# Attention-output pieces in front of the score bursts, and one more piece kept back: a transformer block on one core

## The chip, the cores and the metric

The kernel runs on one core of one Trainium2 chip. The metric is the device time of one execution in microseconds (us), as the median of several runs. Engines: PE is the tensor engine's matmul, PEld its weight loads, DVE the vector engine, ACT the scalar engine, POOL GpSimd, SP the engine that issues the transfers here.

## The reference, cut to what matters

```python
# x: 1 x 2048 x 1024, bf16; 32 heads of 32; causal window of 256
qkv = layernorm(x) @ wqkv
scores = q @ k.T * 32 ** -0.5          # masked: 0 <= query - key < 256
h = x + (softmax(scores) @ v) @ wo
out = h + silu(layernorm(h) @ w1) @ w2 # w1: 1024 x 3584, w2: 3584 x 1024
```

## The kernel before: the parts concerned

The tokens are worked on in four blocks of 512. The dense matmuls of one block (QKV of the next block, or the output projection of the earlier ones) are interleaved with the attention of another, by hooks between single matmuls. A *burst* is a group of 16 to 24 score matmuls on 32-row tiles of the array; ACT then takes their exponentials and POOL sets the masked triangles to zero. A *piece* is 15 to 24 small matmuls (33 columns), which multiply those exponentials by v; DVE divides by the row sums. The last piece of a head schedules a DMA transpose of its output for the start of the next dense group.

The code is shortened here.

```python
class Stream:
    def __init__(self, b):
        self.bursts, self.pieces, self.done, self.given, self.seen = [], [], 0, 0, 0
        self.behind = 2 if b else 1
        pending.extend(coming); coming.clear()      # what the last stream left
        ...                                         # 20 bursts and pieces (16 in block 0)
    def between(self, kt):                          # ahead of each of 192 dense matmuls
        if self.seen * self.n >= self.done * 192:
            self.bursts[self.done]()
            self.done += 1
        if self.seen * self.n * 2 >= (self.given * 2 + 1) * 192:
            if pending:
                pending.pop(0)()
            coming.append(self.pieces[self.given])
            if len(coming) > self.behind:
                pending.append(coming.pop(0))
            self.given += 1
        self.seen += 1
```

Pieces that the last stream leaves over run in the next stage, the first feed-forward matmul, one behind each of its first groups. The projection of block 3 starts in that stage, behind group 6:

```python
run_late()                      # transposes that are due
load_w2(5)
for ft in range(FT):            # here for b == 0; extra: the pieces left over
    acc = h1_group(b, ft)
    run_late()
    if extra:
        extra.pop(0)[0]()
    if b == 0 and ft == 3:
        for i in (1, 2, 3, 4):
            load_w2(i)          # 1 MB each, on SP's queue, as the transposes are
    silu(b, acc, ft)
    if b == 0 and 6 <= ft < 14:
        wo_group(NB - 1, *divmod(ft - 6, 2))   # needs the transposes of all 8 head groups
```

The text calls a head group (four of the 32 heads) a head, as the prediction does: 0 to 7. [...] marks cuts above; the whole kernel may stand here:

The softmax here doesn't subtract the row's maximum and nothing guards it: scores larger than these inputs give would overflow.

## Time and profile before

| | before |
|---|---|
| time, median (the first three runs) | 693.31 us (693.14 to 693.49) |
| span of the profiled run | 691.4 us |
| PE busy, share of the span | 677.0 us, 98% |
| share of PE in the chain that ended last | 97% |
| waits of PE after the first 54 us | none with another engine as releaser |
| last small piece of the streams, start of the next stage | 285.01, 286.48 us |

The rows of the tensor engine at the end of the last stream, in front of those that the prediction shows (start, length, engine, line, operation, out<-in, shape, count):

```profile
283.56 0.43 PE L308 MATMUL sc<-r_a 32*64 32x320 bf16 x24
284.15 1.03 PE L276 MATMUL acc<-r_o,r_a 128*128 128x512 bf16 x4 [0.16 <-issue]
285.01 0.76 PE L388 MATMUL o_ps<-r_a,r_e 128*128 128x33 bf16 x24
285.61 1.02 PE L276 MATMUL acc<-r_o,r_a 128*128 128x512 bf16 x4
```

In the rows `sc` marks a burst, `o_ps` a piece, and `acc` or `hacc` dense matmuls. Read them by their starts: the modelled length of a dense matmul is 379 ns, but the next one starts after 215, so that lengths overlap. For the same reason an idle time shown in brackets behind a dense matmul is 0.16 us shorter than what was lost. The `[0.16 <-issue]` above is no such wait: there the record of one matmul is missing.

### The profile page before, as it was taken

Reading aid. Unit: us, or ns where it says so; the run is one execution under the profiler, and the core shown is the slowest. Engines: PE = TensorE matmul, PEld = TensorE weight load, DVE = VectorE, ACT = ScalarE, POOL = GpSimd, SP = SyncE. Lnnn points to the kernel's source line nnn. Section 1 sums busy time; section 2 is a strip of 40 time slices with the busy share of each in tenths; the row PEclk is TensorE's granted clock in tenths of the full one; section 3 lists DMA queues with packets and bytes.
Section 4 is the critical chain, followed back from the end, with each engine's and each line's share of the span. In section 5 each row is a group of like instructions: output and inputs, shape, how many; then the busy total and the mean of one; then the engine's idle time right before and its main releaser. Section 6 shows DMA issues by size and latency. Waiting matters only on the chain.

```text
span 691.4 us, 14107 instructions
## 1 busy us (share of the span) xinstructions
PE 677.0 (98%) x5895; PEld 331.6 (48%) x6011; DVE 290.5 (42%) x609; ACT 241.8 (35%) x463; POOL 160.4 (23%) x295
## 2 busy tenths in 40 slices
PE   8999999999999999999999999999999999999998
PEld 3444455555555555544444444444444444444445
DVE  5267646744444439534315133343133251333111
ACT  5326666766666666421310033300133100233000
POOL 1007666656666666500000000000000000000000
PEclk9999999999999999999999999999999999999999
DMA  8732242136241889971023410022300024100110
GB/s 251 251 55 78 39 80 61 26 63 183 73 131 17 241 235 281 213 277 50 12 80 111 93 39 0 1 91 69 85 0 1 17 95 95 39 1 1 30 39 24
DMA packets 76463, 60.95 MB, mean 88 GB/s; under 512 B 50288, under 2 KB 60528, under 8 KB 76400
## 3 DMA queue, kind: packets, MB, share of 16 engines
q1 hardware_dynamic: 76256, 59.78, 32.0%
q8 instruction: 47, 0.77, 0.5%
q10 hardware_dynamic: 144, 0.26, 0.1%
q14 instruction: 16, 0.13, 0.1%
HBM read 39.85 MB, written 8.39 MB: 70 GB/s over the span
## 4 chain that ended last, share of the span: by engine, by line
PE 97%; issue 1%; DMA 1%; SPq 0%; DVE 0%
PE hacc L628 19%; PE hacc L665 17%; PE acc L255 16%; PE acc L665 10%; PE acc L628 9%; PE acc L245 8%; PE acc L276 7%; PE o_ps L388 5%; PE sc L308 3%; PE hacc L276 1%; DMA r_w<-in_A_wqkv_dram 1%; PE sc L360 1%; PE sc L334 1%; PE tp L223 0%; SPq L135 0%
## 5 line engine op out<-in xcount | busy, mean ns | idle before, releaser
L378 POOL TENSOR_SCALAR_AFFINE_SELECT r_e<-r_e 128x512 bf16<-128x512 bf16 (+1 forms) x288 | 157.4, 561 | 126.6 <-ACT r_e L368 62.7
L665 PEld LDWEIGHTS <-r_a 128*128 128x128 bf16 x952 | 90.9, 98 | 103.0
L628 PEld LDWEIGHTS <-r_w 128*128 128x128 bf16 x896 | 87.4, 98 | 105.0 <-issue 0.2
L665 PE MATMUL hacc<-r_a 128*128 128x512 bf16 (+2 forms) x607 | 121.8, 359 | 0.5
L628 PE MATMUL hacc<-r_e,r_w 128*128 128x512 bf16 x444 | 99.7, 379 | 0.5
L320 ACT ACTIVATE r_e<-sc 128x768 bf16<-128x768 f32 x96 | 78.2, 814 | 48.3 <-PE sc L308 47.6
L637 ACT ACTIVATE r_n<-hacc 128x512 f32<-128x512 f32 x30 | 17.9, 597 | 178.9 <-PE hacc L628 175.5
L665 PE MATMUL acc<-r_a 128*128 128x512 bf16 x329 | 73.5, 379 | 0.4
L255 PEld LDWEIGHTS <-r_w 128*128 128x128 bf16 x512 | 44.2, 97 | 46.1 <-issue 1.0
L255 PE MATMUL acc<-r_t,r_w 128*128 128x512 bf16 x233 | 60.3, 379 | 2.4 <-issue 1.7
L257 DVE CAST r_a<-acc 128x512 bf16<-128x512 f32 x56 | 38.6, 690 | 56.6 <-PE acc L255 43.8
L255 PE MATMUL acc<-r_w 128*128 128x512 bf16 x240 | 58.0, 379 | 1.5 <-issue 0.9
L388 PEld LDWEIGHTS <-r_e 128*128 128x128 bf16 x1440 | 47.4, 96 | 17.9
L276 PE MATMUL acc<-r_o,r_a 128*128 128x512 bf16 x188 | 49.5, 379 | 1.9 <-issue 1.3
L628 PE MATMUL acc<-r_e,r_w 128*128 128x512 bf16 x213 | 48.9, 379 | 0.3
L388 PE MATMUL o_ps<-r_a,r_e 128*128 128x33 bf16 x1440 | 48.1, 178 | 0.1
L321 ACT ACTIVATE r_e<-sc 128x256 bf16<-128x256 f32 x96 | 37.6, 392 | 0.0
L680 DVE SCALAR_TENSOR_TENSOR r_t<-hacc,r_t 128x512 bf16<-128x512 f32 (+2 forms) x22 | 14.0, 635 | 55.2 <-PE hacc L665 53.8
L680 DVE SCALAR_TENSOR_TENSOR r_t<-acc,r_t 128x512 bf16<-128x512 f32 x12 | 8.3, 692 | 64.2 <-PE acc L665 58.8
L638 DVE SCALAR_TENSOR_TENSOR r_a<-r_n,hacc 128x512 bf16<-128x512 f32 x30 | 20.6, 688 | 33.0 <-ACT r_n L637 33.0
L628 PE MATMUL hacc<-r_a,r_w 128*128 128x512 bf16 x139 | 32.6, 379 | 0.3
L276 PEld LDWEIGHTS <-r_a 128*128 128x128 bf16 x256 | 21.8, 97 | 22.3
(79 smaller groups left out, 532.5 us busy)
## 6 DMA issues: line engine op xcount, KB each, us to landing
r_w<-in_B_w_dram SPq DMA_DIRECT2D x8, 896.0 KB, 5.2
r_a<-in_B_w_dram SPq DMA_DIRECT2D x7, 1024.0 KB, 7.5
r_w<-in_A_wqkv_dram SPq DMA_DIRECT2D x6, 1024.0 KB, 9.3
h_dram<-r_t SPq DMA_DIRECT2D x16, 256.0 KB, 2.5
r_t<-h_dram SPq DMA_DIRECT2D x16, 256.0 KB, 2.9
out_dram<-r_t SPq DMA_DIRECT2D x31, 128.0 KB, 1.7
r_o<-in_A_x_dram SPq DMA_DIRECT2D x15, 256.0 KB, 4.2
r_e<-h_dram SPq DMA_DIRECT2D x3, 1024.0 KB, 5.7
```

The source lines that it names most:

```text
L245: nc.tensor.matmul(acc, lhsT=lnT_b[b % 2][:, kt, j * P:(j + 1) * P], rhs=wv[:, kt, c * 512:(c + 1) * 512], start=(kt == 0), stop=(kt == KT ...
L255: nc.tensor.matmul(acc, lhsT=wqk[:, kt, col0:col0 + P], rhs=lnT_b[b % 2][:, kt, :], start=(kt == 0), stop=(kt == KT - 1))
L257: copy(out=(qT, kT)[which][b][:, g, :], in_=acc)
L276: nc.tensor.matmul(acc, lhsT=qT[b][:, g, j * P:(j + 1) * P], rhs=wo[:, g, c * 512:(c + 1) * 512], start=(g == 0), stop=(g == G - 1))
L308: nc.tensor.matmul(sc[hh // 2][half * 64:half * 64 + 64, hh % 2, col:col + qb - qa], lhsT=kT[t // 4][r0:r0 + DH, g, k0:k0 + 64], rhs=qT[b] ...
L320: nc.scalar.activation(out=tri[:, :, :, 64:256], in_=both, func=ACT.Exp, scale=scale)
L321: nc.scalar.activation(out=e[:, 1024:1280].rearrange("p (h q) -> p h q", q=P), in_=bank[:, :, 192:320], func=ACT.Exp, scale=scale)
L378: nc.gpsimd.affine_select(out=dst, in_=src, pattern=[[0, n] for n in dst.shape[1:-1]] + [[sgn, P]], compare_op=ALU.is_ge if upper else ALU ...
L388: nc.tensor.matmul(o_ps[pair][:, qt * 2 + hh, 0:VW], lhsT=chunk_of(i, bank, piece, pair, hh), rhs=v[:, b * 4 + kt, g * 4 + pair * 2 + hh, ...
L628: nc.tensor.matmul(acc, lhsT=w1[:, kt, ft * P:(ft + 1) * P], rhs=ln2T[b][:, kt, :], start=(kt == 0), stop=(kt == KT - 1))
L665: nc.tensor.matmul(acc[:, 0:c1 - c0], lhsT=gT[:, ft, j * P:(j + 1) * P], rhs=w2[ft // 4][:, ft % 4, c0:c1], start=(ft == 0), stop=(ft == F ...
L680: nc.vector.scalar_tensor_tensor(out=t_out[j % 2][:, c0:c1], in0=acc[:, 0:c1 - c0], scalar=0.5, in1=t_in[j % 2][:, c0:c1], op0=ALU.mult, o ...
```

## The change

The intent is to have fewer changes of kind on the tensor engine: each piece directly in front of a burst. With the position alone each piece would run half a slot sooner after its burst (3 slots, not 3.5), so it is kept back by one more.

```diff
-            self.behind = 2 if b else 1
+            self.behind = 3 if b else 2
 ...
             if self.seen * self.n >= self.done * 192:
-                self.bursts[self.done]()
-                self.done += 1
-            if self.seen * self.n * 2 >= (self.given * 2 + 1) * 192:
                 if pending:
                     pending.pop(0)()
-                coming.append(self.pieces[self.given])
+                self.bursts[self.done]()
+                coming.append(self.pieces[self.done])
                 if len(coming) > self.behind:
                     pending.append(coming.pop(0))
-                self.given += 1
+                self.done += 1
             self.seen += 1
```

More of the change, by code (lines that the diff above doesn't have):

```diff
@@ L424, in __init__ @@
         def __init__(self, b):
-            self.bursts, self.pieces, self.done, self.given, self.seen = [], [], 0, 0, 0
-            self.behind = 2 if b else 1
+            self.bursts, self.pieces, self.done, self.seen = [], [], 0, 0
+            self.behind = 3 if b else 2
             pending.extend(coming)
```

## The prediction

> **What bounds the kernel now.** I read four views in this order: the page (who is busy), the chain that ended last (what sets the end), the list of waits (is there one that a new order could remove), and then the timeline of the tensor engine inside a stretch where the change acts.
>
> From the page, engine totals and the chain:
>
> ```profile
> PE 677.0 (98%) x5895; PEld 331.6 (48%) x6011; DVE 290.5 (42%) x609; ACT 241.8 (35%) x463; POOL 160.4 (23%) x295
> ...
> PE 97%; issue 1%; DMA 1%; SPq 0%; DVE 0%
> ```
>
> The matmul engine is busy for 98% and 97% of the chain lies on it, so only what the tensor engine itself does, or waits for, counts. In the list of waits the longest entries belong to ACT, DVE and POOL, which wait for PE. For PE there is almost nothing after the start ("PE acc L255 <- issue" 2.7 us in 17 times; 0.16 us each, where the rows beside it lack one matmul, so I read these as missing records). So there is no wait to win. What is left is the cost of changing from one kind of matmul to another. The timeline of PE, two slots of it (columns: start, length, engine, line, operation, out<-in, shape, count):
>
> ```profile
> 200.35 0.38 PE L255 MATMUL acc<-r_t,r_w 128*128 128x512 bf16 x1
> 200.56 0.61 PE L388 MATMUL o_ps<-r_a,r_e 128*128 128x33 bf16 x18
> 201.03 1.24 PE L255 MATMUL acc<-r_t,r_w 128*128 128x512 bf16 x5
> 202.19 0.43 PE L308 MATMUL sc<-r_a 32*64 32x320 bf16 x24
> 202.78 0.81 PE L255 MATMUL acc<-r_t,r_w 128*128 128x512 bf16 x3 [0.16 <-issue]
> 203.43 0.54 PE L388 MATMUL o_ps<-r_a,r_e 128*128 128x33 bf16 x15
> 203.81 1.24 PE L255 MATMUL acc<-r_t,r_w 128*128 128x512 bf16 x5
> 204.99 0.43 PE L308 MATMUL sc<-r_a 32*64 32x320 bf16 x24
> ```
>
> Read start to start, since lengths overlap. Five dense matmuls in a row last 1.24 us with the last one 0.379 us long, so one starts every (1.24-0.38)/4 = 0.215 us. Dense to piece: three from 202.78 put the next start at 203.43, as found (203.43): no loss. Piece to dense: 18 small ones from 200.56 to 201.03 are 0.026 us each, 15 from 203.43 to 203.81 are 0.025: no loss either. Dense to burst: the fifth dense matmul started at 201.03+4x0.215 = 201.89 and would free the array at 202.11; the burst starts at 202.19, 0.09 us later. The same on 203.81: 204.89 against 204.99. Only entering a burst (and leaving it) costs something; a piece between dense matmuls is free of transition cost.
>
> **What the Trainium skill says.** "TensorE: Matmul & The Clock Gate", Step-by-step: what each phase is for: weight loads are pulled ahead of running matmuls if the row groups don't conflict or they go to the background buffer. The trace agrees for dense and piece (0.215 and 0.025 us, no gap) and shows that a burst's first load of a 32-row tile is not hidden (0.09 us). Same page, What's actually happening: a window of about 3.4 us without matmuls drops the clock to half. This trace has no idle gap of that length; it shows only the cold state at the start (the 11 warm-up matmuls take 632 ns in the mean against 379 later). "DMA: Bandwidth & Descriptors", Queues, rings and completion order: on each DMA engine the descriptors of one ring are taken in ring order, and a completion count lands only after all earlier writes of that engine. The trace agrees: an attention transpose issued right behind two 1 MB weight loads and two 256 KB ones landed after 8.7 us; one with a free queue takes 2.4 us (issued at 165.97 and 293.81):
>
> ```profile
> r_a<-r_n SPq DMA_TRANSPOSE x1, 8.7
> ```
> ```profile
> r_a<-r_n SPq DMA_TRANSPOSE x1, 2.4
> ```
>
> **The change part by part.** (a) Order. Before, a slot is burst, dense, piece, dense; after, piece, burst, dense. Piece p ran 3.5 slots behind its burst p, now 4 (blocks 1 to 3; 2.5 to 3 in block 0). Between two bursts there is therefore the same piece as before: burst k to burst k+1 held piece k-3 at k+0.5 and holds piece (k+1)-4 = k-3 now. So the time that ACT has to empty the score banks before the next burst is unchanged (it uses about 2.7 us of at least 2.79), and bursts stay where they were. No instruction is added or removed: 12,024 rows on PE in both.
>
> (b) Transitions. Per slot one dense-to-burst (0.215+0.09) and one piece-to-dense (0.026) are replaced by one piece-to-burst and one dense-to-dense (0.215). The loss of 0.09 us goes with entering the tiled mode, not with what ran before: leaving the burst costs about as much (a burst of 24 from 204.99 takes 0.35 us to the next dense start at 205.34, though its last matmuls have 64 columns). So piece-to-burst should be 33 columns at the dense rate, 0.215x33/512 = 0.014, plus 0.094, 0.108 us: 0.108+0.215-0.305-0.026 = -0.01 us. Of the 76 pieces, 13+19+20+20 = 72 still run in the four streams: 72 x -0.01 = -0.6 us in all.
>
> (c) The tail. Keeping back one more piece leaves four, not three, behind the last stream: the second half of head 6 (24 matmuls) and the three of head 7 (15, 18, 15). They run after the first four dense groups of the next stage. The transpose of head 7 is issued at the start of the group after its last piece, now the fifth group and no longer the fourth. But in the fourth group the program issues four 1 MB loads of the second weight. The instruction orders of the two kernels set side by side show it: on SP the row "transpose, then four loads" has become "four loads, then transpose". Output projection of block 3 needs that transpose at the eighth matmul of its first group, after seven groups. Before, timelines of PE and SP:
>
> ```profile
> 286.48 1.89 PE L628 MATMUL acc<-r_a,r_w 128*128 128x512 bf16 x8
> 288.20 0.53 PE L388 MATMUL o_ps<-r_a,r_e 128*128 128x33 bf16 x15
> ...
> 299.78 1.89 PE L276 MATMUL hacc<-r_o,r_a 128*128 128x512 bf16 x8
> ```
> ```profile
> 293.81 1.20 SPq L408 DMA_TRANSPOSE r_a<-r_n  x1
> 295.05 2.75 SPq L619 DMA_DIRECT2D r_a<-in_B_w_dram  x4
> ```
>
> First, the stage's start. The piece of 24 leaves the stream (24x0.0254 = 0.61 us), so the stage could begin at 286.48-0.61 = 285.87. But its first weight load needs the last of four layer-norm transposes, which was issued at 282.86 and landed after 3.3 us, at 286.2; I take 286.3, a loss of 0.4 us. Then the need: seven groups of 8x0.2155 (12.07), four pieces of 72 small matmuls (1.83) and seven matmuls (1.51) later: 286.3+15.4 = 301.7. (The same sum with three pieces gives 299.77 for the start of the first projection group before; the trace has 299.78.)
>
> When is it ready? Head 6's piece ends at 286.3+1.72+0.61 = 288.6; before, its transpose followed a piece by 0.94 us (292.87 to 293.81), so 289.6, and SP is free for the first of the four loads 1.24 us later, at 290.8. The last load waits on SP for the last piece, at about 295, which does not matter as the three before it fill the queue. Before, the last of the four landed 14.9 us after the issue of the first (296.82+13.1-295.05):
>
> ```profile
> r_a<-in_B_w_dram SPq DMA_DIRECT2D x1, 1024.0 KB, 13.1
> ```
>
> That gives 305.7, and 0.4 more for the transpose (in the case of 8.7 us it landed 0.4 after the load ahead of it): 306.1, a stall of 4.4 us. By the rate in the flat part of the DMA row (about 390 GB/s: 10.8 us for four, with 2.3 us before the first bytes and 0.6 for the transpose) it is ready at 304.5, a stall of 2.8. I take the middle, 3.6 us. PE works in order, has no slack afterwards, and nothing gives this back. A gap of this length may also just let the clock drop for one window; I estimate 1.7 us at a chance of about one in eight, 0.2.
>
> Sum: 693.3 - 0.6 + 0.4 + 3.6 + 0.2 = 696.9 us, +0.5%.
>
> **The rivals.** (1) The weight load of the burst hides under the small matmuls, and piece-to-burst costs 0.026 like piece-to-dense. Then 72 x 0.09 = 6.5 us are saved and the result is 691 us. For it: it is the obvious purpose of the change. Against it: leaving a burst costs the same 0.09 us although short matmuls precede. (2) The transposes don't stall: the loads may be issued early enough, or the first group may be late. Then about 693. Against it stand the 8.7 us above. (3) The pieces come later against ACT, POOL and DVE, and rings or banks fill: a score ring is freed by a piece one place in front of the burst that refills it, on the same engine, so the refill never waits; and waits for POOL's masks become shorter. I give it nothing. (4) The stall is long enough to cool the clock for longer, or the queue is slower than 280 GB/s: 699 to 701.
>
> **Range and chances.** The tail alone (2.8 to 4.4) gives 696.1 to 697.7; rival 1 in part and rival 2 pull down to 693, rival 4 up to 700: 693.0 to 699.8. A change of 2% would be 13.9 us. Saving that is twice what all transitions cost; losing it needs a queue twice as slow. Faster 0.01, same 0.97, slower 0.02.
>
> **What would show it.** In the changed profile: the first projection group of block 3 (the one at 299.78 before) is split by an idle of about 3.6 us whose releaser is a DMA into r_a from r_n; SP shows the four loads ahead of that transpose, which takes about 10 us to land; the stream's rows show piece to burst at 0.11 us start to start; bursts keep their times up to 283.6 within 1 us. The prediction is wrong if the burst follows the last small matmul after 0.03 us, or if no DMA wait stands before the projection.

## The result, and the profile after

The changed kernel took 699.27 us (699.0 to 699.84, 4 runs) against 693.24 us (4 runs): ratio 1.0089, 95% interval 1.0074 to 1.0103. A ratio here is the mean time of one kernel's runs over that of the other's in the same rounds, so it isn't quite the ratio of the medians. Its result is correct. It is 6.0 us slower; 3.6 were forecast.

Engine totals and the chain of the changed kernel, from its page:

```profile
PE 678.5 (97%) x5896; PEld 342.6 (49%) x6011; DVE 291.6 (42%) x609; ACT 241.8 (35%) x463; POOL 160.8 (23%) x295
...
PE 96%; DMA 2%; issue 1%; SPq 0%; DVE 0%
```

PE does the same work; the DMA share of the chain has gone from 1% to 2% (the page lists the new 1% as `DMA r_a<-r_n`, an attention transpose). First the streams, at the place that the prediction showed:

```profile
201.47 0.61 PE L388 MATMUL o_ps<-r_a,r_e 128*128 128x33 bf16 x18
202.01 0.43 PE L308 MATMUL sc<-r_a 32*64 32x320 bf16 x24
202.59 1.89 PE L255 MATMUL acc<-r_t,r_w 128*128 128x512 bf16 x8 [0.16 <-issue]
204.32 0.54 PE L388 MATMUL o_ps<-r_a,r_e 128*128 128x33 bf16 x15
204.79 0.43 PE L308 MATMUL sc<-r_a 32*64 32x320 bf16 x24
```

18 small matmuls at 0.0255 would put the burst at 201.93 if it followed as another small one does; it starts at 202.01, 0.08 later. In the trace's start times, the 72 steps from a last small matmul to a burst took 106 to 111 ns, against 309 to 312 from a dense one and 25 to 27 from a small matmul to a dense one (both in the kernel before). By these steps one slot gains 0.309+0.026-0.216-0.108 = 0.011 us, 0.8 us in 72 slots; the streams as a whole show less. The last burst of the streams began at 283.56 before and begins at 283.17 now; the first at 50.54 and 50.72. That makes -0.57 us over the streams, and +0.18 from the program's start, in which executions differ. The -0.57 is firm: from first to last burst the changed kernel and runs 1, 5, 6 and 7 took 232.45 us each, the kernel before and run 2 took 233.02. Where the other 0.2 of the 0.8 went I can't say.

Now the tail, tensor engine:

```profile
283.75 1.89 PE L276 MATMUL acc<-r_o,r_a 128*128 128x512 bf16 x8 [0.16 <-issue]
286.10 1.89 PE L626 MATMUL acc<-r_a,r_w 128*128 128x512 bf16 x8 [0.46 <-issue]
287.82 0.76 PE L388 MATMUL o_ps<-r_a,r_e 128*128 128x33 bf16 x24
...
300.00 1.68 PE L276 MATMUL hacc<-r_o,r_a 128*128 128x512 bf16 x7
305.89 0.39 PE L276 MATMUL hacc<-r_o,r_a 128*128 128x512 bf16 x1 [4.22 <-DMA r_a<-r_n]
306.12 2.81 PE L626 MATMUL hacc<-r_a,r_w 128*128 128x512 bf16 x8
```

and SP, with the time that the transpose issued at 295.71 took to land:

```profile
289.35 1.20 SPq L408 DMA_TRANSPOSE r_a<-r_n  x1
290.60 4.57 SPq L617 DMA_DIRECT2D r_a<-in_B_w_dram  x4
295.71 3.44 SPq L408 DMA_TRANSPOSE r_a<-r_n  x1
```
```profile
r_a<-r_n SPq DMA_TRANSPOSE x1, 10.1
```

The stage begins late (0.46 shown, 0.62 lost), the projection's first seven matmuls run, and the eighth waits for the transpose: 4.6 us from the seventh to the eighth, where 0.22 are due, so 4.38 lost. Then eight dense matmuls last 2.81 us and no longer 1.89: from 306.93 on they run at half the clock. The engines' shares in three stretches of the length of one clock record (stretch, its length, busy us of PE, PEld, DVE, ACT, POOL with counts, granted clock, DMA share, GB/s):

```profile
300.10:303.52 3.42, 1.57 (x8) 0.49 (x5) 0.69 (x1) 0.60 (x1) 0.00 (x0) 1.00 1.04 384
303.52:306.93 3.41, 1.04 (x5) 0.51 (x6) 0.61 (x1) 0.00 (x0) 0.00 (x0) 1.00 0.56 181
306.93:310.35 3.42, 3.42 (x9) 1.18 (x8) 0.77 (x2) 0.60 (x1) 0.00 (x0) 0.50 0.02 5
```

In the first two, PE is idle for more than half; the third is busy throughout but at 0.50. The kernel before in the same stretch ran 17 matmuls in place of 9:

```profile
306.93:310.35 3.42, 3.42 (x17) 1.54 (x16) 1.38 (x2) 0.56 (x2) 0.00 (x0) 1.00 0.53 196
```

3.41 us at half speed lose 1.70. The account: -0.57 (streams) +0.18 (start) +0.62 (late start of the stage) +4.38 (transpose) +1.70 (clock) = +6.31; the profiled spans are 691.4 and 697.7 us.

### The profile page after: what moved, and what is told of

The parts are those of the page before. It is cut to its first block, busy times and chain, and to the rows that moved or that the text cites. A ratio compares the mean times of both kernels' runs of the same rounds, so it can differ in the third digit from the quotient of the medians.

```text
span 697.7 us, 14110 instructions
## 1 busy us (share of the span) xinstructions
PE 678.5 (97%) x5896; PEld 342.6 (49%) x6011; DVE 291.6 (42%) x609; ACT 241.8 (35%) x463; POOL 160.8 (23%) x295
## 4 chain that ended last, share of the span: by engine, by line
PE 96%; DMA 2%; issue 1%; SPq 0%; DVE 0%
PE hacc L626 18%; PE hacc L663 17%; PE acc L255 16%; PE acc L663 10%; PE acc L626 9%; PE acc L245 8%; PE acc L276 6%; PE o_ps L388 5%; PE sc L308 2%; DMA r_a<-r_n 1%; PE hacc L276 1%; DMA r_w<-in_A_wqkv_dram 1%; PE sc L360 1%; PE sc L334 1%; PE tp L223 0%
## 5 line engine op out<-in xcount | busy, mean ns | idle before, releaser
L663 PEld LDWEIGHTS <-r_a 128*128 128x128 bf16 x952 | 90.9, 98 | 103.0
L626 PEld LDWEIGHTS <-r_w 128*128 128x128 bf16 x896 | 87.4, 98 | 105.7 <-issue 1.6
L255 PEld LDWEIGHTS <-r_w 128*128 128x128 bf16 x512 | 47.1, 98 | 55.0 <-issue 1.0
L255 PE MATMUL acc<-r_t,r_w 128*128 128x512 bf16 x233 | 56.5, 380 | 2.4 <-issue 1.7
L255 PE MATMUL acc<-r_w 128*128 128x512 bf16 x240 | 56.0, 379 | 1.5 <-issue 0.9
L276 PE MATMUL acc<-r_o,r_a 128*128 128x512 bf16 x188 | 46.3, 380 | 1.9 <-issue 1.3
L276 PEld LDWEIGHTS <-r_a 128*128 128x128 bf16 x256 | 23.7, 99 | 32.5 <-DMA r_a<-r_n 4.7
```

The source lines that it names most:

```text
L255: nc.tensor.matmul(acc, lhsT=wqk[:, kt, col0:col0 + P], rhs=lnT_b[b % 2][:, kt, :], start=(kt == 0), stop=(kt == KT - 1))
L276: nc.tensor.matmul(acc, lhsT=qT[b][:, g, j * P:(j + 1) * P], rhs=wo[:, g, c * 512:(c + 1) * 512], start=(g == 0), stop=(g == G - 1))
L626: nc.tensor.matmul(acc, lhsT=w1[:, kt, ft * P:(ft + 1) * P], rhs=ln2T[b][:, kt, :], start=(kt == 0), stop=(kt == KT - 1))
L663: nc.tensor.matmul(acc[:, 0:c1 - c0], lhsT=gT[:, ft, j * P:(j + 1) * P], rhs=w2[ft // 4][:, ft % 4, c0:c1], start=(ft == 0), stop=(ft == F ...
```

## The experiments

Theory: the loss lies in the tail alone, and is made by the order on SP's queue, which keeping back one more piece has turned round; the clock adds to it. Rivals are stated with each run. Ratios are against the kernel before in the same rounds (693.15 us for runs 1 to 4 and 693.31 us for runs 5 to 7, the medians of nine runs each; the two sets ran on different chips).

**1. The loads behind the transpose again.** The changed kernel, but

```diff
-            if b == 0 and ft == 3:
+            if b == 0 and ft == 4:
                 for i in (1, 2, 3, 4):
                     load_w2(i)
```

> The changed kernel, with the four loads of the second weight issued one dense group later, so that the transpose of head 7 stands ahead of them on the queue again, as before the change. Theory (the queue order costs the time): no idle of PE before the projection of block 3, the transpose lands in 2.4 to 3 us, the clock stays at 1.0; left are -0.6 us from transitions and +0.5 us at the stage's start: 693.2 us, 692.8 to 693.6. Rival (it is the later work itself, four pieces in the tail instead of three, that delays the transpose): the stall stays for the larger part, 696 us or more.

Measured: 693.24 us (692.46 to 693.59, 5 runs), ratio 1.000 (0.9987 to 1.0012). The clock was 1.0 in all five. Its PE and SP rows:

```profile
299.70 1.89 PE L276 MATMUL hacc<-r_o,r_a 128*128 128x512 bf16 x8
```
```profile
289.05 7.60 SPq L408 DMA_TRANSPOSE r_a<-r_n  x2
296.70 2.40 SPq L617 DMA_DIRECT2D r_a<-in_B_w_dram  x4
```

Both transposes stand ahead of the loads and the projection runs in one piece. Four pieces remain in the tail, so they are not the cause: the rival falls, and the 6 us hang on the order of these transfers. What is left of the change, the gain of the streams and the late start of the stage, cancels.

**2. The order on the queue alone, in the kernel before.** Here nothing of the change is present; only the loads are issued ahead of the transpose.

```diff
             acc = h1_group(b, ft)
+            if b == 0 and ft == 3:
+                for i in (1, 2, 3, 4):
+                    load_w2(i)
             run_late()
             if extra:
                 extra.pop(0)[0]()
-            if b == 0 and ft == 3:
-                for i in (1, 2, 3, 4):
-                    load_w2(i)
```

> The kernel before, with nothing changed but that the four loads are issued ahead of head 7's transpose in the same group. Theory: the transpose waits behind 4 MB. The first load can go as soon as head 6's transpose and a write are out, about 290.0, the last lands some 15 us later at 305, the transpose 0.4 later; PE needs it at 301.3: a stall of about 4 us and, as in the changed kernel, one window of half clock of 3.4 us, which costs 1.7: 698.5 to 699.5 us. Rival (the order of the pieces, not of the queue): 693.3.

Measured: 700.5 us (699.67 to 700.71, 4 runs), ratio 1.0103 (1.0089 to 1.0117), 1 us above the expected range.

```profile
306.00 0.61 PE L276 MATMUL hacc<-r_o,r_a 128*128 128x512 bf16 x1 [4.95 <-DMA r_a<-r_n]
306.40 3.62 PE L628 MATMUL hacc<-r_a,r_w 128*128 128x512 bf16 x8
```

The stall was 5.1 us (5.33 between the starts, of which 0.22 are due) where I expected about 4: the transpose landed at 305.95, 0.5 later than I had reckoned, and PE needed it 0.4 sooner, at 300.9. In three of four runs the mean clock was 0.995, in the fourth, the shortest (699.67), 0.998: in the profiled one the half clock lasted 6.8 us, two stretches, not one. Order alone makes the loss, and more of it.

**3. One half of the change: the position, without keeping back one more.**

```diff
-            self.behind = 3 if b else 2
+            self.behind = 2 if b else 1
```

(on the changed kernel).

> One half of the change: each piece directly in front of a burst, but kept back by no more pieces than before, so piece p runs 3 slots after burst p instead of 3.5 and three pieces are left for the tail. Theory: no stall in the tail. But the piece in front of burst 3 of a pair reads what burst 2 has written, one slot (3 us) earlier; ACT needs 2.7 us of that, and POOL's four masks some 0.6 us each after it; PE waits for POOL up to 1 or 2 us in some slots of each pair, 12 pairs: 697 to 712 us. Rival (the order alone brings the gain, the further distance is not needed): 692.7 us, with no wait of PE for POOL.

Measured: 701.15 us (701.02 to 701.55, 4 runs), ratio 1.0115 (1.0102 to 1.0129). No stall in the tail, the clock at 1.0 or 0.999. Its list of waits (who waited for whom: us in total, times, longest):

```profile
PE o_ps L388 <- POOL r_e L378: 4.9, 23, 0.5
```

23 waits of PE for POOL's masks, all inside a piece, with 0.15 us each that the list doesn't count (length against spacing of small matmuls): 4.9 + 23x0.153 = 8.4 us, which the start times give too. The gain of the streams off, 7.8 are left; the run is 8.0 longer. The time is in the range that I gave, and POOL is what PE waits for, but more often and for less than I wrote: no wait was near 1 to 2 us (the longest shows 0.5, 0.6 by the starts). The rival (the position alone brings the gain) falls: without the extra distance the pieces come too soon after their bursts.

**4. The other half: keep back one more, without the position**, with the loads moved as in run 1.

```diff
-            self.behind = 2 if b else 1
+            self.behind = 3 if b else 2
 ...
-            if b == 0 and ft == 3:
+            if b == 0 and ft == 4:
```

(on the kernel before).

> The other half: pieces half way between two bursts as before, but kept back by one more, and the four loads moved behind the transpose so that the tail does not stall. Piece 4 of a pair then runs half a slot after the burst whose exponentials overwrite what it reads. Theory: ACT waits for that piece, about 1.4 us into the slot, ends its 2.4 us of work 0.8 to 1.2 us after the next burst could begin, and PE waits for ACT so much in one to three slots of each pair: 12 pairs, 12 to 35 us more: 705 to 728 us. Rival (distance does no harm): 693.3 us with no such wait.

Measured: 759.65 us (758.79 to 760.27, 4 runs), ratio 1.0954, and the **result is wrong** (relative error 0.54), which I hadn't intended. My reason was wrong too. I took it that ACT would wait for a late piece. But the piece stands in the program behind the burst whose exponentials overwrite what it should read. The order of the program decides which of them waits: the piece reads the new data, and PE waits for ACT and POOL to make it.

```profile
PE o_ps L388 <- POOL r_e L378: 19.1, 34, 1.1
PE o_ps L388 <- ACT r_e L321: 11.9, 11, 1.1
PE o_ps L388 <- ACT r_e L342: 10.3, 12, 0.9
```

So the two parts of the change belong together: the position in front of the burst is the last place at which one more piece of distance is still allowed. As a time it says nothing about a legal kernel. The trace showed one thing more. The clock fell to half in ten stretches of 3.41 us, though no two matmuls started more than 1.5 us apart in the streams. The stretch before the first drop, and the drop:

```profile
142.27:145.68 3.41, 1.73 (x31) 0.73 (x10) 2.32 (x7) 2.06 (x4) 2.98 (x6) 1.00 0.03 5
145.68:149.09 3.41, 2.75 (x38) 1.24 (x39) 0.63 (x2) 0.00 (x0) 0.38 (x1) 0.50 0.16 33
```

PE had been busy for half of the stretch, in several parts.

**5. The projection one group later**, on the changed kernel: the transpose is needed 1.72 us later.

```diff
-            if b == 0 and 6 <= ft < 14:
-                j, c = divmod(ft - 6, 2)
+            if b == 0 and 7 <= ft < 15:
+                j, c = divmod(ft - 7, 2)
```

> The changed kernel, with the output projection of block 3 beginning one dense group (1.72 us) later. Theory: the transpose lands at the same time, about 305.9 us, so PE's idle shrinks from 4.2 to 2.5 us. If the clock still drops for one window: 697.5; if a gap of 2.5 us does not drop it: 695.8 us. Rival (the wait is no race against a fixed landing): the idle stays at 4 us and the time at 699.3.

Measured: 697.11 us (695.12 to 697.53, 5 runs), ratio 1.0048 (1.0035 to 1.0061). The five fall into two kinds: 695.12 and 696.13 us with a clock of 1.0, and 697.11, 697.50 and 697.53 with 0.998, the share of one stretch at half clock. The means differ by 1.75 us, close to the 1.70 worked out above for one stretch, in one and the same kernel; but these are two runs against three, and the two lie 1.0 us apart. The profile is of the 695.12 run. It holds no clock record; that its clock was full is seen from the eight dense matmuls behind the wait, which took 1.89 us. For the 696.13 run this couldn't be checked.

```profile
304.90 0.39 PE L276 MATMUL hacc<-r_o,r_a 128*128 128x512 bf16 x1 [1.62 <-DMA r_a<-r_n]
```

The idle shrank to 1.6 us, somewhat more than by one group (I expected 2.5); the transpose landed at 304.86 here, 1 us earlier than in the changed kernel. The runs with the dropped clock were not profiled, so their idle isn't known.

**6. The projection two groups later.**

```diff
-            if b == 0 and 6 <= ft < 14:
-                j, c = divmod(ft - 6, 2)
+            if b == 0 and 8 <= ft < 16:
+                j, c = divmod(ft - 8, 2)
```

> The same with two dense groups (3.45 us) later. Theory: an idle of 0.8 us is left, the clock stays at 1.0: 694.1 us (693.24 - 0.6 + 0.5 + 0.8 = 693.9, with 0.2 for the start). Together with the run of one group later and the changed kernel this gives the size of the clock's part: the time falls by more than the idle does, by 1.7 us, at the step where the drop vanishes.

Measured: 694.01 us (693.54 to 694.08, 5 runs), ratio 1.0008 (0.9995 to 1.002), clock 1.0 in all.

```profile
305.03 0.39 PE L276 MATMUL hacc<-r_o,r_a 128*128 128x512 bf16 x1 [0.68 <-DMA r_a<-r_n]
```

Later need, smaller idle: it is a race against a nearly fixed landing (305.85 us in the changed kernel, 304.86 in run 5, 304.98 here). From the profiled execution of the changed kernel to this one the span fell by 6.0 us: 3.5 of idle, 1.7 of clock, 0.5 because the stage began only 0.1 us late here, and 0.3 from the program's start.

**7. The first of the pieces left over run ahead of the stage**, on the changed kernel.

```diff
+    pending.pop(0)()
     run_late()
     load_w2(5)
```

> The changed kernel, with the first of the four pieces left over run in front of the next stage's first dense group, not behind it. Theory: it fills the 0.46 us in which PE waits for the layer-norm transpose, only three pieces remain in the stage, so head 7's transpose is ahead of the four loads as before the change; no idle, clock 1.0, and what is left is the gain from transitions: 692.6 us, 692.3 to 693.0, faster than both kernels by 0.1%. Rival (nothing is gained by the new order in the streams): 693.2.

Measured: 692.52 us (692.40 to 692.76, 5 runs), ratio 0.9988, interval 0.9974 to 1.0001. By the interval this is the same as before; but all five lie below all nine runs of the kernel before (692.90 to 693.75), and the size, -0.8 by the medians and -0.5 by the profiled spans, is about the -0.57 of the streams. Its rows:

```profile
285.41 0.76 PE L388 MATMUL o_ps<-r_a,r_e 128*128 128x33 bf16 x24
286.01 1.89 PE L626 MATMUL acc<-r_a,r_w 128*128 128x512 bf16 x8
```

The piece now fills the time in which the stage waited for the layer-norm transpose, with no idle behind it, and the last transpose is ahead of the loads again. Between this and run 1 lie 0.72 us (0.88 if each is taken against the kernel before of its own set), and 0.4 between their profiled spans; the late start in run 1's own trace is 0.54. It differs between executions of the changed order: 0.62 in the changed kernel, 0.89 in run 5, 0.1 in run 6, each time with the first matmul 0.2 us after the last layer-norm transpose landed.

## Why the prediction was right, and where it was off

It gave 696.9 us and a range of 693.0 to 699.8; 699.27 is within it, near its upper end. The main account (the tail alone) ended at 697.7, so the result lies beyond it and in the band of the prediction's rival 4, 699 to 701. Of that rival the clock came true; the queue was not slower than reckoned. So the mechanism, the wait and its place were forecast; that the range held is owed to the rival. By its own terms:

- **Transitions, -0.6.** Measured -0.57. Piece to burst took 108 ns in the median of 72, the figure that it had worked out from the way out of a burst. That the sums agree so closely is in part luck: its -0.008 per slot comes from rounded steps, and the measured steps would give 0.8. Rival 1 (the load hides, -6.5 us) fell.
- **Start of the stage, +0.4.** Measured +0.62. The last layer-norm transpose landed at 285.90, 0.3 sooner than I took, and the first matmul came 0.2 after it, not 0.1. But PE itself was ready at 285.48 and not at 285.87, as the gain of the streams lets it wait earlier: part of that gain was lost again here.
- **Transpose behind the loads, +3.6.** Measured +4.38. There were two estimates, 4.4 from the landing of the four loads before and 2.8 from the flat rate. The first was right: landing forecast at 306.1, found at 305.85. Taking the middle cost 0.8 us. One reading was loose: the queue was not quite free for the transpose at 293.81 (a 1 MB load landed at 295.65), but run 1's, with nothing in flight, took 2.4 us as well.
- **Clock, +0.2.** This is the term that was mis-sized. The step was that a gap of that length "may also just let the clock drop for one window", one time in eight. I had asked for a stretch of 3.4 us without any matmul. The mean clock was 0.998 or lower in each of the four runs: at least one stretch at half clock, 1.7 us. The traces of the changed kernel (PE busy for 1.04 of 3.41 us ahead of the drop) and of run 4 show that a stretch that is partly idle is enough.
- **Distance and rings, nothing.** Right: bursts kept their times within 0.4 us and no engine but the queue made PE wait. Runs 3 and 4 show how narrow this was: one piece less costs 8 us, one place more gives a wrong result.

Is the clock's stretch a fixed one, and how little work makes it fall? In the eight traces with a clock record every change lies a whole number of stretches of 3.413 us after the first record (in run 4 the drops last one, with 5 or 10 between them): in these runs it goes by fixed stretches. An estimate of the limit from the start times: count each matmul up to the next start, at most 0.216 us for a dense and 0.026 for any other one. Then the twelve stretches in front of a drop held 0 to 1.27 us of matmuls, and no other stretch at full clock less than 1.40. So where a stall falls among the stretches can decide whether it costs 1.7 us more; that this is what divides the five runs of run 5 is likely, but not shown. What stays open is the exact limit, and what counts towards it: some records are missing, and if dense matmuls alone are counted the two groups overlap.

## What to carry to other kernels

When a change delays work by a step, follow what that work issues last, here one transpose, and look at what now stands ahead of it on its queue; 4 MB of loads that were harmless behind it cost 4.4 us ahead of it. On an engine that is always busy, a stall can cost more than its length, because the clock can fall too: here 4.4 us became 6.1, while the 0.7 us of run 6 left the clock alone. And when work is moved between stages, its new place can be chosen: run 7 filled an existing wait with it, without moving anything else.

## What the Trainium skill lacked or had wrong

- "TensorE: Matmul & The Clock Gate", What's actually happening and HAM oscillation, tie the drop to an idle window of about 3.4 us. Here it fell after a 4.2 us gap of which no stretch of 3.41 us, as the clock's record cuts them, was wholly idle (PE busy 1.57 and 1.04 us), and in run 4 after stretches like that with PE busy for 1.73 of 3.41 us and no gap above 1.5 us between two starts. The same page tells, further down, of a clock that swings because of many short idle times, but not how much work in a window is too little; the runs put it between 1.27 and 1.40 us (the estimate above). The 3.41 us of half clock and the fixed stretches agree with the page.
- The same page, Part 3, says what overlaps between tiles of different row groups, and "TensorEngine Tiling (Array Packing)" says that a change of tiling mode drains the engine; neither says what entering the tiled mode costs beside full-array matmuls: 309 ns start to start after a 512-column matmul (216 without), 108 after a 33-column one (25 without); 0.08 to 0.09 us each. The runs don't tell a drain from a weight load that isn't hidden.
- "DMA: Bandwidth & Descriptors", Queues, rings and completion order, is right on ring order, and no page draws the warning from it: the same small transpose landed after 2.4 us with nothing in flight (run 1) and after 10.1 us behind 1 MB loads (the changed kernel).
- "Perfetto Trace Analysis" says that the profiler estimates a matmul's end; it doesn't add that an idle time shown behind one is therefore too short, by modelled length less spacing: 0.16 us behind a dense matmul (379 and 215 ns), 0.15 behind a small one (178 and 25), which was 3.5 of 8.4 us in run 3.
